# Stage A of six batches on quarters of TensorE

## The chip, the cores and the metric

The kernel runs on one core of one Trainium2 chip. The metric is the device time of one execution in microseconds (us). The kernel before takes 795.54 us, the median of three runs from 795.02 to 796.49 us.

## What is computed

```python
x: (8, 3008, 256)            # batch, sequence, dim
X = np.fft.rfft(x, axis=1)   # along the 3008 rows of each batch
Y = X * (filt_r + 1j * filt_i)
y = np.fft.irfft(Y, n=3008, axis=1)
h = np.maximum(y.reshape(24064, 256) @ w_in, 0.0)   # w_in: 256 x 2048
out = (h * h) @ w_out                               # w_out: 2048 x 256
```

The Fourier transform is done as matmuls. 3008 is 64 times 47, so a batch is first transformed over 47 rows for each of 64 residues n1 ("stage A", into u), then over the 64 residues ("stage B", psB), multiplied by the filter, and brought back in two steps (psP, psY). The two dense layers (psH, then psO) follow.

## The kernel before

Stage A of a batch has a 94-row contraction: the residues n1 are split in two halves h of 32, and a row of the tile x is a pair (n2, h) with n2 below 47. The constant SA holds the cosines and sines of 47 rows twice, each only in the rows of its own h, so half of the 94 x 96 constant is zero. One matmul takes 94 rows, 96 columns and two values of m (512 elements).

```python
for c in range(NC):                       # NC = 24
    for h in range(2):
        SA[:, h, h, 0, c] = np.cos(2 * np.pi * n2 * c / N2)
        SA[:, h, h, 1, c] = np.sin(2 * np.pi * n2 * c / N2)
...
p_x32 = ctx.enter_context(tc.tile_pool(name="p_x32", bufs=2))
p_x16 = ctx.enter_context(tc.tile_pool(name="p_x16", bufs=4))
p_u = ctx.enter_context(tc.tile_pool(name="p_u", bufs=3))
...
def psF(name):
    return pps.tile([128, 512], F32, tag="psF", name=name, bufs=2)
...
def load_x(b, c, pool=None, tag="x32", q=None):
    t = (pool or p_x32).tile([96, 8, D], F32, tag=tag, name=f"x32_{b}_{c}")
    ...                                    # one transfer, two for the last batch
def cast_x(b, c, eng=nc.vector):
    t = p_x16.tile([94, 8, D], F16, tag="x16", name=f"x16_{b}_{c}")
    eng.tensor_copy(out=t, in_=x32s.pop((b, c))[0:94])
    x16s[(b, c)] = t

def write_u(b, c):
    nc.sync.dma_start(
        out=dU[b].rearrange("(m q) d -> q m d", q=96)[:, 8 * c:8 * c + 8, :],
        in_=us.pop((b, c)))

def unit_a(b, a):
    c, i = divmod(a, 4)
    if i == 0:
        us[(b, c)] = p_u.tile([96, 8, D], F16, tag="u", name=f"u_{b}_{c}")
    ps = psF(f"psA_{b}_{a}")
    m = slice(2 * i, 2 * i + 2)
    if b == 1:
        ...                                # batch 1: another layout of x
    else:
        nc.tensor.matmul(ps[0:96, :], sSA, x16s[(b, c)][:, m, :], start=True, stop=True)
    o = us[(b, c)][:, 2 * i:2 * i + 2, :]
    pv = ps[0:96, :].rearrange("p (a d) -> p a d", d=D)
    if a % 2 == 0:
        nc.scalar.copy(out=o, in_=pv)
    else:
        nc.vector.tensor_copy(out=o, in_=pv)
    if i == 3:
        write_u(b, c)
```

u goes out to DRAM (dU) and comes back in another order (ut) for stage B. The main loop has one step for every eighth of a group of 512 tokens. In each step TensorE does the matmuls of the first layer, then what the plan puts in place 0, then the matmuls of the second layer, then place 1:

```python
# fft_plan(b): steps count from the start of the plan of batch b
t0 = 2 if b == 1 else 6
for a in range(12 if b == 1 else 0, 16):
    put(t0 + a // 2, a % 2, unit_a, b, a)          # batches 2 to 7: steps 6 to 13
put(10 if b == 1 else 14, 1, read_u, b)            # dU -> ut
t0 = 14 if b == 1 else 18
for p in range(12):
    r = t0 + (18 if b == 1 else 19) * p // 11
    put(r, 0, unit_b, b, p)                        # stage B from step 18
    ...
for s in range((NG + 1) * SLOTS):
    g, k = divmod(s, SLOTS)
    if g < NG:
        ffn_g1(g, k)          # psH: 4 matmuls of 512 columns; ScalarE: relu into h
    run(work, s, 0)
    if g > 0:
        ffn_g2(g - 1, k)      # psO: 8 matmuls of 256 columns
    run(work, s, 1)
    if g > 0:
        ffn_out(g - 1, k)     # every fourth step: ScalarE copies psO out
    if g < NG:
        ffn_sq(g, k)          # VectorE: h * h
```

Of the kernel before, what the change touches and what calls it, by code (L numbers as in the profile page):

```python
# [9 lines left out]
F16 = mybir.dt.float16  # L10
F32 = mybir.dt.float32
# [7 lines left out]
N1, N2, NC, NM = 64, 47, 24, 32  # L19
# [7 lines left out]
def _build_consts():  # L27
    N = N1 * N2
    n2 = np.arange(N2)
    m = np.arange(NM)  # L30


    SA = np.zeros((N2, 2, 2, 2, NC))
    for c in range(NC):
# [6 lines that stand above are left out]
    S0 = np.zeros((128, 6, 2, 48))  # L41
    for h in range(2):
        q = SA[:, h, h].reshape(N2, 48)
        for t in range(2):
            S0[2 * h + t::4, t, h] = q[:32]
        for c in range(4):
            S0[4 * h + c:120:8, 2 + c, h] = q[32:]


    freq = np.full((NC, 64), -1)  # L50
    for c in range(NC):
        for j in range(32):
            freq[c, j] = 47 * j + c
            if c:
                freq[c, 32 + j] = 47 * j + 47 - c
    freq[0, 32] = N // 2


    SB = np.zeros((NM, 2, 2, NC, 2, 64))

    n1j = 8 * (m % 8) + 2 * (m // 8)
    SP = np.zeros((2, 64, NC, 2, 2, NM))
    for c in range(NC):
        for f in range(64):
            k = freq[c, f]
            if k < 0:
                continue
            sg = 1.0 if (f < 32 or c == 0) else -1.0
            for h in range(2):
                th = 2 * np.pi * ((k * (32 * h + m)) % N) / N  # L70
                SB[:, h, 0, c, 0, f] = np.cos(th)
                SB[:, h, 1, c, 0, f] = -sg * np.sin(th)
                SB[:, h, 0, c, 1, f] = -np.sin(th)
                SB[:, h, 1, c, 1, f] = -sg * np.cos(th)
            if c == 0 and f == 32:
                SB[:, :, 1, c, :, f] = 0.0
            w = (1.0 if k in (0, N // 2) else 2.0) / N
            for i in range(2):
                th = 2 * np.pi * ((k * (n1j + i)) % N) / N
                cs, sn = w * np.cos(th), w * np.sin(th)  # L80
                SP[0, f, c, i, 0] = cs
                SP[0, f, c, i, 1] = sg * sn
                SP[1, f, c, i, 0] = -sn
                SP[1, f, c, i, 1] = sg * cs


    SY = np.zeros((32, 2, 2, N2, 2))
    for c in range(NC):
        th = 2 * np.pi * c * n2 / N2
        for i in range(2):  # L90
            SY[c + c // 12 * 4, i, 0, :, i] = np.cos(th)
            SY[c + c // 12 * 4, i, 1, :, i] = -np.sin(th)


    PF = np.zeros((128, 6, 2, 2, 32))
    for w, (s, q) in enumerate(PQ):
        for j in range(32):
            PF[4 * j + q, w, :, s, j] = 1.0

    f16 = lambda a, p: np.ascontiguousarray(a.reshape(p, -1).astype(np.float16))  # L100
    C0 = np.zeros((128, 1472))
    C0[:, 0:576] = S0.reshape(128, 6, 2, 2, NC).transpose(0, 1, 4, 2, 3).reshape(128, 576)
    C0[:, 576:704] = np.eye(128)
    C0[:, 704:1280] = S0.reshape(128, 576)
    C0[0:94, 1280:1376] = SA.reshape(94, 96)
    C0[:, 1376:1470] = SY.reshape(128, 94)
    return f16(C0, 128), f16(PF, 128), f16(SB, 128), f16(SP, 128)

# [2 lines left out]
def kernel(  # L111
# [9 lines left out]
    nc = tc.nc  # L121
    B, S, D = x.shape
# [17 lines left out]
# [3 lines that stand above are left out]
# [10 lines left out]
    xrows = x.rearrange("b s d -> (b s) d")  # L153
    dU = [dram.tile([NM * 96, D], F16, name=f"dU{b}") for b in range(B)]
    dZ = [dram.tile([NM * 96, D], F16, name=f"dZ{b}") for b in range(B)]

    def psF(name):
        return pps.tile([128, 512], F32, tag="psF", name=name, bufs=2)

    def psO(name):  # L160
        return pps.tile([128, 2, 256], F32, tag="psO", name=name, bufs=2)
# [22 lines left out]
    x32s = {}  # L184

    def load_x(b, c, pool=None, tag="x32", q=None):

        t = (pool or p_x32).tile([96, 8, D], F32, tag=tag, name=f"x32_{b}_{c}")
        q = q or nc.sync
        if b + 1 < B:  # L190
            v = xrows[b * S:b * S + 96 * NM, :].rearrange("(p m) d -> p m d", m=NM)
            q.dma_start(out=t, in_=v[:, 8 * c:8 * c + 8, :])
        else:
            v = xrows[b * S:b * S + S, :].rearrange("(p m) d -> p m d", m=NM)
            q.dma_start(out=t[0:80], in_=v[0:80, 8 * c:8 * c + 8, :])
            q.dma_start(out=t[80:94], in_=v[80:94, 8 * c:8 * c + 8, :])
        x32s[(b, c)] = t


# [1 line left out]
    sC0 = const.tile([128, 1472], F16, name="sC0")  # L201
    nc.scalar.dma_start(out=sC0[:, 0:704], in_=dC0.ap()[:, 0:704])
    s0 = sC0[:, 0:576].rearrange("p (w q) -> p w q", q=96)
    s1 = sC0[:, 704:1280].rearrange("p (w q) -> p w q", q=96)
    sSA = sC0[0:94, 1280:1376]
    sSY = sC0[0:112, 1376:1470]
    ident = sC0[:, 576:704]
    sPF = p_out.tile([128, 6, 128], F16, tag="ost", name="sPF")
# [1 line left out]
    xw32, xw16 = {}, {}  # L210
# [61 lines left out]
    ps = psO("warm").rearrange("p a d -> p (a d)")  # L272
# [61 lines left out]
    x16s, us, uts, prods, zes, zts, yts = {}, {}, {}, {}, {}, {}, {}  # L334

    def cast_x(b, c, eng=nc.vector):
        t = p_x16.tile([94, 8, D], F16, tag="x16", name=f"x16_{b}_{c}")
        eng.tensor_copy(out=t, in_=x32s.pop((b, c))[0:94])  # L338
        x16s[(b, c)] = t

    def write_u(b, c):
        nc.sync.dma_start(
            out=dU[b].rearrange("(m q) d -> q m d", q=96)[:, 8 * c:8 * c + 8, :],
            in_=us.pop((b, c)))

    def unit_a(b, a):

        c, i = divmod(a, 4)
        if i == 0:
            us[(b, c)] = p_u.tile([96, 8, D], F16, tag="u", name=f"u_{b}_{c}")  # L350
        ps = psF(f"psA_{b}_{a}")
        m = slice(2 * i, 2 * i + 2)
        if b == 1:
            nc.tensor.matmul(ps[0:96, :], s1[:, c // 2, :], xw16[(b, 2 * (c % 2))][:, m, :],
                             start=True, stop=False)
            nc.tensor.matmul(ps[0:96, :], s1[0:120, 2 + c, :], xw16[(b, 1)][0:120, m, :],
                             start=False, stop=True)
        else:
            nc.tensor.matmul(ps[0:96, :], sSA, x16s[(b, c)][:, m, :], start=True, stop=True)  # L359
        o = us[(b, c)][:, 2 * i:2 * i + 2, :]  # L360
        pv = ps[0:96, :].rearrange("p (a d) -> p a d", d=D)
        if a % 2 == 0:
# [5 lines that stand above are left out]
# [240 lines left out]
    def fft_plan(b):  # L608

        plan = {}  # L610

        def put(r, place, f, *a):
            plan.setdefault((r, place), []).append((f, a))

        if b == 1:
            for n in range(4, 16):
                put(n if n < 8 else n + 2 if n < 12 else 2 * n - 7, n % 2, unit_y, 0, n)
            for k in range(4):
                put((4, 5, 7, 7)[k], 1, cast_wout, k, nc.vector)
        t0 = 2 if b == 1 else 6  # L620
        for a in range(12 if b == 1 else 0, 16):
            put(t0 + a // 2, a % 2, unit_a, b, a)
        put(10 if b == 1 else 14, 1, read_u, b)
        t0 = 14 if b == 1 else 18
        for p in range(12):
            r = t0 + (18 if b == 1 else 19) * p // 11
            put(r, 0, unit_b, b, p)
            put(r, 0, unit_s, b, p)
            put(r + 2, 1, unit_p, b, p)
        t0 = 35 if b == 1 else 40  # L630
        for c in range(4):
            put(t0, 1, read_z, b, c)
        if b + 1 < B:
            for c in range(2):
                put(t0 - 13, 1, load_x, b + 1, c)
            for c in range(4):
                r = t0 - 8 + 3 * c
                put(r, 1, cast_x, b + 1, c)
                if c < 2:
                    put(r, 1, load_x, b + 1, c + 2)  # L640
        for n in range(16):
            if b == 1:
                put(38 + n // 2 if n > 3 else 39, n % 2, unit_y, b, n)
            else:
                put(44 + n // 2, n % 2, unit_y, b, n)
        return plan
# [16 lines left out]
    for k in range(2):  # L663
        c = slice(12 * k, 12 * k + 12)
# [16 lines left out]
    for k in range(2):  # L681
        sSPx.append(p_u.tile([128, 12, 128], F16, tag="u", name=f"sSPx_{k}"))
        c = slice(12 * k, 12 * k + 12)
# [33 lines left out]
    for c in (0, 2, 1):  # L717
        write_u(1, c)
# [12 lines left out]
    for s in range((NG + 1) * SLOTS):  # L731
        g, k = divmod(s, SLOTS)
# [40 lines left out]
```

## Time and profile before

| what | value |
|---|---|
| time, median of 3 | 795.54 us |
| span of the profiled execution | 795.8 us |
| PE (matmuls) busy | 783.1 us, 98% of the span |
| VectorE (DVE) busy | 552.2 us, 69% |
| ScalarE (ACT) busy | 554.9 us, 70% |
| matmuls of stage A of batches 2 to 7 (psA, line 359) | 96, 382 ns each |
| matmuls of the first layer (psH, line 560) | 1728, 351 ns each |
| matmuls of the second layer (psO, line 577) | 3008, 272 ns each |
| ScalarE's copies of psA to u (line 363) | 50, 572 ns each |
| VectorE's copies of psA to u (line 365) | 50, 687 ns each |
| ScalarE's relu (line 564) | 376, 1025 ns each |

A record of a matmul starts with its reading and has a modelled end, so records of consecutive matmuls overlap: the spacing of their starts, not their length, is what a matmul costs in a full stream. PEld are the loads of the stationary operand. "a <- b" in a row of waits says what the idle engine a waited for.

### The profile page before, as it was taken

How to read it: one execution, taken by the hardware profiler on the slowest of the kernel's cores; microseconds unless marked ns; L12 is line 12 of the kernel's file. 1: busy time of each engine (PE TensorE's matmuls, PEld its weight loads, DVE VectorE, ACT ScalarE, POOL GpSimd, SP SyncE). 2: the span in 40 equal slices, each digit the busy share in tenths (PEclk: the TensorE clock that was granted, in tenths of full speed). 3: DMA queues.
4: the chain of work that ended last, by engine and by line, in shares of the span. 5: the costliest groups of instructions: out<-in, count | busy, mean ns of one | idle time of the engine just before them, and what ended most of it. 6: DMA issues, size and time to landing. Idle time of an engine off the chain costs nothing.

```text
span 795.8 us, 14801 instructions
## 1 busy us (share of the span) xinstructions
PE 783.1 (98%) x6102; PEld 553.7 (70%) x6102; DVE 552.2 (69%) x898; ACT 554.9 (70%) x708; POOL 24.4 (3%) x27
## 2 busy tenths in 40 slices
PE   8989999999999999999999999999999999999998
PEld 5846677667676676867778676776777667776666
DVE  6946995579855897559965699557985589554342
ACT  3856776767777677767777677676776767766664
POOL 3710000000000000000000000000000000000000
PEclk9989999999999999999999999999999999999999
DMA  9994555336724467055471555525563342511111
GB/s 352 361 277 134 130 151 139 92 126 165 202 58 107 158 165 181 30 164 151 124 183 49 171 153 137 129 71 156 156 170 97 87 142 80 123 48 41 40 41 54
DMA packets 88139, 107.32 MB, mean 135 GB/s; under 512 B 6288, under 2 KB 78864, under 8 KB 83856
## 3 DMA queue, kind: packets, MB, share of 16 engines
q1 hardware_dynamic: 87864, 106.19, 46.9%
q8 instruction: 48, 0.79, 0.4%
q10 hardware_dynamic: 144, 0.18, 0.1%
q14 instruction: 19, 0.16, 0.1%
q0 software_dynamic: 64, 0.00, 0.0%
HBM read 58.12 MB, written 48.23 MB: 134 GB/s over the span
## 4 chain that ended last, share of the span: by engine, by line
PE 93%; DMA 3%; ACT 1%; DVE 1%; issue 0%; POOL 0%; SPq 0%; ACTq 0%; DVEq 0%; POOLq 0%
PE psO L577 40%; PE psH L560 39%; PE psA L359 3%; PE psY L530 3%; PE psB L443 2%; PE psP L494 2%; PE warm L274 1%; DMA ut<-dU 1%; DMA xw<-in_x_dram 1%; PE psf L293 1%; DMA dZ<-ze 1%; ACT h L564 1%; PE psf L296 0%; DMA dU<-u 0%; PE psA L380 0%; ACT sF L303 0%
## 5 line engine op out<-in xcount | busy, mean ns | idle before, releaser
L564 ACT ACTIVATE h<-psH 128x1024 f16<-128x1024 f32 x376 | 385.2, 1025 | 189.7 <-PE psH L560 188.2
L577 PE MATMUL psO<-sWout,h 128*128 128x256 f16 x3008 | 388.6, 272 | 0.0
L560 PE MATMUL psH<-yt,sWin 128*128 128x512 f16 (+7 forms) x1728 | 386.9, 351 | 1.7 <-DVE yt L539 0.8
L577 PEld LDWEIGHTS <-h 128*128 128x128 f16 x3008 | 290.6, 98 | 77.3
L568 DVE TENSOR_TENSOR h<-h 128x1024 f16<-128x1024 f16 x376 | 253.7, 685 | 100.8 <-ACT h L564 99.2
L560 PEld LDWEIGHTS <-sWin 128*128 128x128 f16 x1728 | 159.5, 98 | 101.7 <-issue 3.5
L451 DVE TENSOR_TENSOR prod<-psB,sF 128x1024 f16<-128x1024 f32 x84 | 102.4, 1219 | 5.9 <-PE psB L443 5.6
L539 DVE CAST yt<-psY 128x376 f16<-128x376 f32 x62 | 33.9, 549 | 57.4 <-PE psY L530 57.4
L365 DVE CAST u<-psA 96x512 f16<-96x512 f32 x50 | 34.3, 687 | 47.3 <-PE psA L359 45.1
L496 ACT CAST ze<-psP 128x512 f16<-128x512 f32 x84 | 49.2, 586 | 17.8 <-PE psP L494 15.9
L588 ACT COPY ost<-psO 128x512 f32<-128x512 f32 (+1 forms) x96 | 55.7, 580 | 6.7 <-PE psO L577 5.3
L530 PEld LDWEIGHTS <-zt 112*128 112x128 f16 x512 | 34.9, 98 | 12.1 <-issue 2.0
L530 PE MATMUL psY<-sC,zt 112*128 112x94 f16 x512 | 42.3, 205 | 0.6 <-DMA zt<-dZ 0.3
L465 DVE TENSOR_TENSOR yf<-prod,yf 128x512 f16<-128x512 f16 x84 | 35.7, 425 | 2.9
L443 PE MATMUL psB<-ut,sSB 128*128 128x256 f16 x192 | 36.5, 272 | 0.6 <-DMA ut<-dU 0.5
L359 PE MATMUL psA<-x,sC 94*96 94x512 f16 x96 | 36.6, 382 | 0.0
L443 PEld LDWEIGHTS <-sSB 128*128 128x128 f16 x192 | 18.6, 98 | 20.9 <-issue 1.7
L494 PE MATMUL psP<-yf,sSP 128*128 128x256 f16 x168 | 32.1, 273 | 0.2 <-ACT yt L537 0.2
L537 ACT CAST yt<-psY 128x376 f16<-128x376 f32 x66 | 30.7, 468 | 1.1 <-PE psY L530 0.6
L338 DVE CAST x<-x 94x2048 f16<-94x2048 f32 x24 | 29.2, 1216 | 0.0
L363 ACT CAST u<-psA 96x512 f16<-96x512 f32 x50 | 28.6, 572 | 0.0
L458 DVE COPY yf<-prod 64x512 f16<-64x512 f16 x84 | 24.3, 289 | 2.9
(63 smaller groups left out, 255.9 us busy)
## 6 DMA issues: line engine op xcount, KB each, us to landing
x<-in_x_dram SPq DMA_DIRECT2D x20, 768.0 KB
zt<-dZ SPq DMA_DIRECT2D x64, 192.0 KB
dU<-u SPq DMA_DIRECT2D x28, 384.0 KB
dZ<-ze SPq DMA_DIRECT2D x28, 384.0 KB
out_dram<-ost SPq DMA_DIRECT2D x66, 128.0 KB
out_dram<-ost SPq DMA_DIRECT2D x31, 256.0 KB
ut<-dU SPq DMA_DIRECT2D x7, 1024.0 KB
xw<-in_x_dram SPq DMA_DIRECT2D x4, 1024.0 KB
```

The source lines that it names most:

```text
L359: nc.tensor.matmul(ps[0:96, :], sSA, x16s[(b, c)][:, m, :], start=True, stop=True)
L443: nc.tensor.matmul(ps[:, i * D:(i + 1) * D], sSB[:, 2 * p + i, :], uts[b][:, 2 * p + i, :], start=True, stop=True)
L451: nc.vector.tensor_mul(out=prod, in0=ps.rearrange("p (a d) -> p a d", d=D).unsqueeze(1).to_broadcast([128, 2, 2, D]), in1=sF[:, :, 2 * p:2 ...
L465: nc.vector.tensor_add(out=yf, in0=prod[:, 0], in1=yf)
L494: nc.tensor.matmul(ps[:, i * D:(i + 1) * D], sSP[:, 2 * p + i, :], yf[:, i, :], start=True, stop=True)
L496: nc.scalar.copy(out=zes[(b, c)][:, 2 * i6:2 * i6 + 2, :], in_=ps.rearrange("p (a d) -> p a d", d=D))
L530: nc.tensor.matmul(ps[:, 94 * jj:94 * jj + 94], zt[:, 4 * (g % 2) + jj, dt * 128:(dt + 1) * 128], sSY, start=True, stop=True)
L560: nc.tensor.matmul(ps[:, i, o:o + n], sWin[:, dt, jt * 128:(jt + 1) * 128], yts[b][:, dt, r:r + n], start=(dt == 0), stop=(dt == 1))
L564: nc.scalar.activation(out=h2[:, 2 * s:2 * s + 2, :], in_=ps, func=AF.Relu)
L568: nc.vector.tensor_mul(out=v, in0=v, in1=v)
L577: nc.tensor.matmul(pso[g][:, t % 2, :], h2s[g][:, jt, t * 128:(t + 1) * 128], sWout[:, jt, :], start=(jt == 0), stop=(jt == NJT - 1))
L588: nc.scalar.copy(out=ost[:, h0:h0 + step, :], in_=pso[g][:, h0:h0 + step, :])
```

## The change

In batches 2 to 7 the zero half of SA is no longer multiplied. Each half h gets its own 64 rows of the array (rows 0 to 46 and 64 to 110 carry data), and two groups of m go to two halves of the columns (48 of 64 columns carry data). So one pass consists of four matmuls, each on a 64 x 64 quarter of the array, which are meant to run at the same time. A pass computes what two matmuls computed before; there are 8 passes for a batch in place of 16 matmuls. A pass takes both psF buffers, one for each h; ScalarE empties the one, VectorE the other.

For that x is loaded by h: for each of the four chunks two transfers (64 and 48 partitions, 112 in place of 96; the last batch in more pieces), and the cast takes 112 partitions. The tile u has 128 partitions, and write_u makes four transfers of 48 partitions in place of one of 96. In the plan the passes stand in place 0 of steps 6 to 13; place 1 of these steps is empty.

```diff
-    C0[0:94, 1280:1376] = SA.reshape(94, 96)
+    for h in range(2):
+        C0[64 * h:64 * h + N2, 1280:1328] = SA[:, h, h].reshape(N2, 48)
...
-        t = (pool or p_x32).tile([96, 8, D], F32, tag=tag, name=f"x32_{b}_{c}")
+        t = (pool or p_x32).tile([112, 8, D], F32, tag=tag, name=f"x32_{b}_{c}")
...
+        for h in range(2):
+            n = 64 - 16 * h
+            for n0, n1 in ((0, n),) if full else ((0, 32), (32, N2), (N2, n)):
+                a = n0 if full or n0 < N2 else 0
+                q.dma_start(out=t[64 * h + n0:64 * h + n1],
+                            in_=v[h, a:a + n1 - n0, 8 * c:8 * c + 8, :])
...
-    sSA = sC0[0:94, 1280:1376]
+    sSA = sC0[:, 1280:1344]
...
-        t = p_x16.tile([94, 8, D], F16, tag="x16", name=f"x16_{b}_{c}")
-        eng.tensor_copy(out=t, in_=x32s.pop((b, c))[0:94])
+        t = p_x16.tile([112, 8, D], F16, tag="x16", name=f"x16_{b}_{c}")
+        eng.tensor_copy(out=t, in_=x32s.pop((b, c)))
...
+        v = dU[b].rearrange("(m h q) d -> q h m d", h=2, q=48)
+        for k in range(2):
+            for h in range(2):
+                m = 8 * c + 4 * k
+                nc.sync.dma_start(out=v[:, h, m:m + 4, :], in_=u[64 * k:64 * k + 48, h])
+
+    def pass_a(b, a):
+        c, j = divmod(a, 2)
+        if j == 0:
+            us[(b, c)] = p_u.tile([128, 2, 4, D], F16, tag="u", name=f"u_{b}_{c}")
+        ps = [psF(f"psA_{b}_{a}_{h}") for h in range(2)]
+        for k in range(2):
+            for h in range(2):
+                m = 4 * k + 2 * j
+                nc.tensor.matmul(ps[h][64 * k:64 * k + 64, :], sSA[64 * h:64 * h + N2, :],
+                                 x16s[(b, c)][64 * h:64 * h + N2, m:m + 2, :],
+                                 start=True, stop=True)
+        for h, eng in enumerate((nc.scalar.copy, nc.vector.tensor_copy)):
+            eng(out=us[(b, c)][:, h, 2 * j:2 * j + 2, :],
+                in_=ps[h].rearrange("p (a d) -> p a d", d=D))
+        if j == 1:
+            write_u(b, c)
...
-            nc.tensor.matmul(ps[0:96, :], sSA, x16s[(b, c)][:, m, :], start=True, stop=True)
...
-        for a in range(12 if b == 1 else 0, 16):
-            put(t0 + a // 2, a % 2, unit_a, b, a)
+        if b == 1:
+            for a in range(12, 16):
+                put(2 + a // 2, a % 2, unit_a, b, a)
+        else:
+            for a in range(8):
+                put(6 + a, 0, pass_a, b, a)
```

More of the change, by code (lines that the diff above doesn't have):

```diff
@@ L186, in load_x @@
     def load_x(b, c, pool=None, tag="x32", q=None):
-        t = (pool or p_x32).tile([96, 8, D], F32, tag=tag, name=f"x32_{b}_{c}")
+        t = (pool or p_x32).tile([112, 8, D], F32, tag=tag, name=f"x32_{b}_{c}")
         q = q or nc.sync
[L190 to L196, printed above, removed]
+        full = b + 1 < B
+        v = xrows[b * S:b * S + (64 if full else N2) * 64, :].rearrange(
+            "(n h m) d -> h n m d", h=2, m=NM)
+        for h in range(2):
[4 more added lines that the diff above has]
+                            in_=v[h, a:a + n1 - n0, 8 * c:8 * c + 8, :])
         x32s[(b, c)] = t
@@ L336, in cast_x @@
     def cast_x(b, c, eng=nc.vector):
-        t = p_x16.tile([94, 8, D], F16, tag="x16", name=f"x16_{b}_{c}")
-        eng.tensor_copy(out=t, in_=x32s.pop((b, c))[0:94])
+        t = p_x16.tile([112, 8, D], F16, tag="x16", name=f"x16_{b}_{c}")
+        eng.tensor_copy(out=t, in_=x32s.pop((b, c)))
         x16s[(b, c)] = t
     def write_u(b, c):
-        nc.sync.dma_start(
-            out=dU[b].rearrange("(m q) d -> q m d", q=96)[:, 8 * c:8 * c + 8, :],
-            in_=us.pop((b, c)))
+        u = us.pop((b, c))
+        if b == 1:
+            nc.sync.dma_start(
+                out=dU[b].rearrange("(m q) d -> q m d", q=96)[:, 8 * c:8 * c + 8, :], in_=u)
+            return
+        v = dU[b].rearrange("(m h q) d -> q h m d", h=2, q=48)
[19 more added lines that the diff above has]
+            write_u(b, c)
     def unit_a(b, a):
@@ L352, in unit_a @@
         m = slice(2 * i, 2 * i + 2)
[L353 to L359, printed above, removed]
+        nc.tensor.matmul(ps[0:96, :], s1[:, c // 2, :], xw16[(b, 2 * (c % 2))][:, m, :],
+                         start=True, stop=False)
+        nc.tensor.matmul(ps[0:96, :], s1[0:120, 2 + c, :], xw16[(b, 1)][0:120, m, :],
+                         start=False, stop=True)
         o = us[(b, c)][:, 2 * i:2 * i + 2, :]
@@ L619, in fft_plan @@
                 put((4, 5, 7, 7)[k], 1, cast_wout, k, nc.vector)
-        t0 = 2 if b == 1 else 6
-        for a in range(12 if b == 1 else 0, 16):
-            put(t0 + a // 2, a % 2, unit_a, b, a)
+        if b == 1:
+            for a in range(12, 16):
[3 more added lines that the diff above has]
+                put(6 + a, 0, pass_a, b, a)
         put(10 if b == 1 else 14, 1, read_u, b)
```

## The prediction

> **What bounds the kernel now.** I read the busy times first, then the slices of the span, the waits of TensorE, and the chain that ended last around one stage A. The page's first part, and from its second the slices of TensorE and of the clock granted to it:
>
> ```profile
> PE 783.1 (98%) x6102; PEld 553.7 (70%) x6102; DVE 552.2 (69%) x898; ACT 554.9 (70%) x708; POOL 24.4 (3%) x27
> ...
> PE   8989999999999999999999999999999999999998
> ...
> PEclk9989999999999999999999999999999999999999
> ```
>
> TensorE is busy everywhere, at full clock. Its waits are few; after the prologue these two kinds matter, half a microsecond each:
>
> ```profile
> PE psH L560 <- DVE yt L539: 0.8, 2, 0.5
> PE psB L443 <- DMA ut<-dU: 0.5, 1, 0.5
> ```
>
> So a nanosecond of TensorE's stream is a nanosecond of the whole, wherever no new wait appears. The chain of work (start us, us, what) shows a step just after the stage A of batch 2, and steps of the stage A of batch 3:
>
> ```profile
> 159.45 0.87 PE psO L577 x8
> 160.33 0.86 PE psH L560 x4
> 161.19 0.87 PE psO L577 x8
> ...
> 243.77 0.22 PE psA L359
> 243.99 0.88 PE psO L577 x8
> 244.87 0.22 PE psA L359
> 245.08 0.86 PE psH L560 x4
> 245.95 0.22 PE psA L359
> 246.17 0.88 PE psO L577 x8
> ```
>
> Without stage A a step lasts 161.19 - 159.45 = 1.74 us; with it 246.17 - 243.99 = 2.18 us. Two matmuls of psA are the difference, 0.44 us, 0.218 us each. All of stage A that changes is 96 x 0.218 = 20.9 us, or 2.6% of 795.8. This is the sum at stake, and half of it, 10.5 us or 1.3%, is what four quarters running perfectly together could save.
>
> **What the Trainium skill says.** "TensorEngine Tiling (Array Packing)", section Key Properties, says that tiles work independently, but that a change of the tiling mode drains TensorE. Every pass stands alone between psH and psO on the whole array, so there are two changes a pass, 96 in all. The trace before has no pass in tiles, hence no price for this. "TensorE: Matmul & The Clock Gate", section Measured speedup vs the span model, gives 3.07 times for four row tiles and 2.38 for three column tiles, so both kinds of tile do run together, not perfectly. The same page, section The mechanism, says that a weight load overlaps running matmuls only where the row groups differ; in a pass the third load has the row group of the first matmul. No run here shows that yet. The first page, section PSUM Bottleneck, says that tiling does not speed up the emptying of PSUM. The trace agrees that its price goes with elements per partition: 572 ns on ScalarE and 687 on VectorE for 512, and the change leaves 512.
>
> **The change part by part.**
>
> Removed: 96 psA matmuls, -20.9 us.
>
> Added: 48 passes of four matmuls of 512 columns. The streaming of one is 0.216 us (0.86 / 4 of a psH group). Four of them together: with the skill's 3.07, 4 x 0.216 / 3.07 = 0.28 us, an estimate. To that come two changes of mode. A psA record is 382 ns long and its neighbour starts 218 ns later, so 0.16 us of a matmul's record lie beside the next one; a full drain would lay this bare at each change, 0.33 us a pass. I take about 0.06 us at each change, since the wavefront itself should be shorter than the record's tail and part of the reading may be early; this is a choice, not a reading. A pass is then 0.28 + 0.12 = 0.40 us, 48 of them 19.2 us. Sum on TensorE: 19.2 - 20.9 = -1.7 us.
>
> The weight loads rise from 96 to 192, but are within the pass estimate.
>
> Beside TensorE: the copies of psA stay 48 on each engine at 572 and 687 ns, with 128 partitions in place of 96. In a step of stage A ScalarE has 1025 + 572 = 1.60 us, and every fourth step 590 ns more for ost, 1.75 us on the average. A step of 1.74 + 0.40 = 2.14 us holds that, and even 1.97 us, the shortest. A pass needs both psF buffers; the relu starts 0.04 us after the pass's start and takes 1.02, then u 0.57, so ScalarE frees its buffer about 1.6 us after the pass began, before the next pass at 2.1. No new wait. The casts of x take the same elements per partition (1216 ns, 24 times). x grows from 768 to 896 KB a chunk, about 0.4 us of transfer at the 361 GB/s of the page's second slice, well ahead of its use: the plan loads the chunks 26 to 18 steps before stage A and casts them 21 to 12 steps before.
>
> On the path: u. In batch 3 the chain leaves TensorE between stage A and B:
>
> ```profile
> 253.57 0.23 PE psA L359
> ...
> 253.83 0.70 DVE u L365
> ...
> 254.59 3.45 DMA dU<-u
> ...
> 258.44 3.63 DMA ut<-dU
> ...
> 262.11 0.38 PE psB L443 x2
> ```
>
> There is no slack there: stage B's first matmuls wait for ut. After the change the last pass stands where psA stood at 252.48 us. ScalarE's relu and copy of u end 1.53 us later (254.01 in the trace), so the writes start about 0.5 us earlier. But they are four of 96 KB, issued 0.3 us apart on SyncE, so the last is issued 1.0 us after the first. The large one carried data from about 0.85 to 2.9 us after its issue, so four small ones should land 3.4 to 3.9 us after the first. Then 0.4 + 3.63 us as before: ut is there at 252.48 + 1.6 + 3.65 + 4.05 = 261.8 us. TensorE gets to stage B at 252.48 + 0.40 + 5 x 1.74 = 261.6 us. The wait of batch 3 becomes 0.2 us from 0.5, and in the other batches, where now there is hardly any, it could be 0 to 0.4. I add 0.5 us for the six. "DMA: Bandwidth & Descriptors", section Rules for kernel authors, holds that transfers to disjoint halves of the partitions serialize; that speaks for no gain from the split, and no run here shows it.
>
> Sum: -1.7 + 0.5 = -1.2 us, 794.3. Because a perfect overlap is as thinkable as a bad one and the change's own purpose speaks for the first, I say 793.8.
>
> **The rivals.** (1) Changes of mode cost nothing: a pass is 0.23 us, 48 x (0.23 - 0.436) = -9.9 us, 785.6. For it: the trace's weight loads lie wholly beside running matmuls (a psO group of 8 takes 0.87 us with its 8 loads). Against: the skill's drain. (2) Full drains laid bare at both ends: 0.28 + 0.33 = 0.61 us, +8.4 us, 803.9; with one weight load bare after each change (98 ns for a full one, 123 for the psA's) 0.82 us, +18 us, 814. For it: the skill's word, and 0.16 us of tail in the records. (3) The second pair on the other columns waits for the first, because their row groups are the same: 2 x 0.216 in place of 0.28, +0.15 us a pass, +7 us on top of mine, 801. (4) Four small writes take longer than one, and ut comes later by 1 us in each batch: +6 us, 800. For it: there is no slack. Against: the bytes are the same and SyncE's issues are short.
>
> **Range and chances.** The low end is rival 1, the high end rival 2 without bare loads and some of rival 4: 785.5 to 806. A gain over 2% (below 779.6) is more than half of stage A and out of reach of the arithmetic: 0.01. A loss over 2% (above 811.4) needs drains and loads bare in all 96 changes, or two rivals together: 0.05. Within 2%: 0.94.
>
> **What would show it.** In the profile after, the spacing of psO groups in stage A: 2.14 us by my step, 1.97 by rival 1, 2.35 to 2.56 by rival 2. The starts of the four matmuls of a pass: within 0.1 us of one another by mine, in two pairs 0.2 us apart by rival 3. Waits of psB on ut above 1 us in total would be rival 4. A wait of psA on ScalarE or VectorE would prove the buffer step wrong. Steps outside stage A must stay at 1.74 us; if they don't, the whole reckoning is wrong.

## The result

The changed kernel takes 816.16 us (median of 4 runs, 815.16 to 817.08), the kernel before 796.01 us beside it. The ratio is 1.025, with a 95% interval of 1.0225 to 1.0275: slower by more than 2%. The prediction was 793.8 us, 785.5 to 806.0.

The page of the changed kernel, first and second part:

```profile
PE 786.9 (97%) x6198; PEld 545.7 (67%) x6198; DVE 556.5 (68%) x898; ACT 555.2 (68%) x708; POOL 24.2 (3%) x27
...
PE   8989999999999999999999999999959999999998
...
PEclk9999999999999999999999999999988999999999
```

One slice of TensorE has fallen to 5, and the clock dips behind it. The span is 813.5 us, a slice is 20.3 us, so this lies near 600 us. TensorE's waits (engine line waited for: us in total, times, longest us):

```profile
PE psY L558 <- DMA zt<-dZ: 7.6, 6, 5.1
PE psO L605 <- DVE h L596: 5.0, 1, 5.0
PE psB L471 <- DMA ut<-dU: 1.4, 3, 0.7
```

Two single waits of 5 us are new. The wait of psO on VectorE was in nobody's list. And the steps of stage A, at which the change was aimed? The timeline of TensorE (start us, us, what), batch 3:

```profile
248.75 0.38 PE L588 MATMUL psH<-yt,sWin 128*128 128x512 f16 x1
249.06 0.41 PE L368 MATMUL psA<-x,sC 47*64 47x512 f16 x4
249.41 1.05 PE L605 MATMUL psO<-sWout,h 128*128 128x256 f16 x8
...
251.59 1.05 PE L605 MATMUL psO<-sWout,h 128*128 128x256 f16 x8
```

The step lasts 251.59 - 249.41 = 2.18 us, as before. The pass is exactly as dear as the two matmuls that it replaced. The four matmuls, 400 ns each in the records, together span 0.41 us: they start within 0.01 us. But the last psH starts at 248.75 and the pass only at 249.06, 0.31 us later in place of 0.216; and psO starts 0.35 us after the pass, again in place of 0.216.

So stage A brought nothing, and the loss is elsewhere. The first psA of the six batches tells where. Those of batches 6 and 7, in the changed kernel and then in the kernel before (count, least/median/greatest ns, first and last start us):

```profile
L368 PE MATMUL psA<-x,sC x32: 400/400/400, 523.7 to 539.0; 47*64 47x512 f16 x32
L368 PE MATMUL psA<-x,sC x32: 400/400/400, 635.0 to 650.3; 47*64 47x512 f16 x32
...
L359 PE MATMUL psA<-x,sC x16: 381/382/382, 522.8 to 539.2; 94*96 94x512 f16 x16
L359 PE MATMUL psA<-x,sC x16: 381/381/381, 618.3 to 634.6; 94*96 94x512 f16 x16
```

From batch 6 to batch 7 it is 635.0 - 523.7 = 111.3 us, before it was 618.3 - 522.8 = 95.5. That is 15.8 of the 17.7 us by which the spans differ. The chain of work in that stretch leaves TensorE altogether:

```profile
567.79 15.66 DMA x<-in_x_dram
...
587.64 12.07 DMA x<-in_x_dram
...
600.14 8.15 DMA dZ<-ze
...
608.31 3.38 DMA zt<-dZ
...
611.83 0.47 PE psY L558 x4
```

It is the load of x of the last batch, which has shapes of its own: the rows behind n2 = 46 don't exist there, and the change fills partitions 47 to 63 from the batch's first rows, in one transfer of 17 partitions a chunk. VectorE, TensorE and then the DMA, from the timelines and from the busy times by stretch:

```profile
597.44 1.23 DVE L343 CAST x<-x 112x2048 f16<-112x2048 f32 x1 [6.54 <-DMA x<-in_x_dram]
...
606.80 1.23 DVE L343 CAST x<-x 112x2048 f16<-112x2048 f32 x1 [6.33 <-DMA x<-in_x_dram]
```

```profile
599.33 1.21 PE L605 MATMUL psO<-sWout,h 128*128 128x256 f16 x4 [5.01 <-DVE h L596]
600.33 1.91 PE L588 MATMUL psH<-yt,sWin 128*128 128x512 f16 x4
602.04 1.91 PE L605 MATMUL psO<-sWout,h 128*128 128x256 f16 x8
...
611.83 0.47 PE L558 MATMUL psY<-sC,zt 112*128 112x94 f16 x4 [5.08 <-DMA zt<-dZ]
```

```profile
core 0: us, PE busy (x) PEld busy (x) DVE busy (x) ACT busy (x) POOL busy (x), PEclk, DMA share, GB/s
592.00:595.00 3.00, 2.32 (x17) 1.46 (x15) 0.00 (x0) 2.35 (x3) 0.00 (x0) 1.00 0.07 25
601.00:604.00 3.00, 3.00 (x12) 1.66 (x11) 0.00 (x0) 1.02 (x1) 0.00 (x0) 0.50 0.47 152
...
610.00:620.00 10.00, 8.17 (x54) 5.55 (x55) 2.29 (x4) 2.77 (x4) 0.00 (x0) 0.66 0.77 149
```

VectorE stood 6.5 us before a cast, because x was not there; behind the cast in its queue were three squarings of h, and psO needed the first. From 592 to 595 us the transfers moved 25 GB/s at a mean share of 0.07 of 16 engines: one engine, 1/16, at work alone, while VectorE and then TensorE waited for it. The packet records of the stretch say the same: packets of 8 KB one at a time, a new one every 0.31 us. After the 5 us of idling TensorE had half its clock (0.50 from 601 to 604 us): from the four psH at 600.33 to the psO at 602.04 it took 1.71 us in place of 0.86. The same happened again after the wait for zt (mean clock 0.66 from 610 to 620 us). The two waits of 5.0 and 5.1 us leave 5.7 of the 15.8 us for the slow matmuls behind them. That agrees with the clock records: half clock for 6.8 us each time, of which TensorE worked 4.9 and 6.0, so 5.5 us were lost.

The second wait has the same source as far as the trace tells. The last chunk's piece was on its way from 599.4 to about 606 us, again a packet of 8 KB every 0.31 us, and VectorE's next cast waited 6.3 us for it; in the same time the write of dZ, which zt reads, took 8.15 us to land. That this write stood behind the piece is a reading and not a test; the second run below removes both waits together.

"DMA: Bandwidth & Descriptors" of the Trainium skill, section Why a DMA increments its semaphore by 16 and not by 1, states the rule that fits: a transfer is spread over the largest number of engines up to 16 that divides the slowest dimension of both its sides. By that rule 17 partitions give one engine. The trace agrees: a share of 0.07, one packet at a time, and 17 rows of 8 KB, 139 KB, take 5.6 us at 25 GB/s.

### The profile page after: what moved, and what is told of

It is laid out like the page before. It is cut to its first block, busy times and chain, and to the rows that moved or that the text cites. A ratio compares the mean times of both kernels' runs of the same rounds, so it can differ in the third digit from the quotient of the medians.

```text
span 813.5 us, 15179 instructions
## 1 busy us (share of the span) xinstructions
PE 786.9 (97%) x6198; PEld 545.7 (67%) x6198; DVE 556.5 (68%) x898; ACT 555.2 (68%) x708; POOL 24.2 (3%) x27
## 4 chain that ended last, share of the span: by engine, by line
PE 79%; DMA 14%; DVE 3%; ACT 2%; SPq 1%; issue 1%; POOL 0%; ACTq 0%; DVEq 0%; POOLq 0%
PE psO L605 34%; PE psH L588 32%; DMA x<-in_x_dram 4%; DMA dZ<-ze 4%; PE psY L558 3%; DMA zt<-dZ 3%; DMA ut<-dU 2%; PE psB L471 2%; PE psP L522 2%; PE psA L368 2%; PE warm L279 1%; DMA xw<-in_x_dram 1%; DVE h L596 1%; ACT h L592 1%; DMA dU<-u 1%; DVE prod L479 1%
## 5 line engine op out<-in xcount | busy, mean ns | idle before, releaser
L372 DVE CAST u<-psA 128x512 f16<-128x512 f32 x48 | 33.2, 692 | 36.4 <-PE psA L368 36.2
L343 DVE CAST x<-x 112x2048 f16<-112x2048 f32 x24 | 29.3, 1222 | 14.7 <-DMA x<-in_x_dram 14.6
L372 ACT CAST u<-psA 128x512 f16<-128x512 f32 x48 | 27.9, 580 | 0.0
L486 DVE COPY yf<-prod 64x512 f16<-64x512 f16 x84 | 24.3, 290 | 2.9
L487 DVE COPY yf<-prod 64x512 f16<-64x512 f16 x84 | 24.2, 288 | 1.1
```

The costliest lines, as they stand in the source:

```text
L372: eng(out=us[(b, c)][:, h, 2 * j:2 * j + 2, :], in_=ps[h].rearrange("p (a d) -> p a d", d=D))
```

## Experiments

**Theories.** A: the last batch's pieces of 17 partitions cost the time. B: the passes and their changes of mode cost it. C: the number of small transfers does. On the pass itself there are two theories as well: 0.22 us of streaming and 0.22 us for two changes of mode, or four quarters that don't really run together.

**1. The last batch without filler** (e1). The filler, the rows behind n2 = 46, is left out; no matmul reads it. The cast is two of 47 partitions.

```diff
-            for n0, n1 in ((0, n),) if full else ((0, 32), (32, N2), (N2, n)):
+            for n0, n1 in ((0, n),) if full else ((0, 32), (32, N2)):
```

> The changed kernel, but the last batch's x is loaded without the filler rows (pieces of 17 partitions and of 1 partition left out; 4 transfers a chunk in place of 6), and its cast is two of 47 partitions. Theory A, the filler pieces hold up the queue and with it batch 7: the 111 us between the first psA of batch 6 and that of batch 7 fall to about 96, the wait of psO on VectorE (5.0 us) and the long one of psY on zt (5.1 us) go, and the time is 795 to 801 us. Theory B, the passes themselves and their mode changes cost the 20 us: the time stays above 812 us. Theory C, the 15-partition pieces or the number of transfers does it: between, 804 to 812 us.

Measured: 801.21 us, ratio to before 1.0068 (1.0039 to 1.0098). Theory B falls. The two waits of 5 us are gone, and the stretch from batch 6 to batch 7 is 98.7 us; both this and the time lie just above what theory A gave (about 96 us, 795 to 801 us). Two waits of psP on VectorE's yf (1.9 us in total) come with the second cast, which costs VectorE 1.2 us a chunk; the third and fourth run, which have one too, show the same 1.9 us.

**2. The same filler, 17 cut into 1 and 16** (e2). The bytes stay, the transfers become more.

```diff
-            for n0, n1 in ((0, n),) if full else ((0, 32), (32, N2), (N2, n)):
+            for n0, n1 in ((0, n),) if full else ((0, 32), (32, N2), (N2, 48), (48, 64))[:4 - h]:
```

> The changed kernel with the same filler rows in the last batch, but the piece of 17 partitions cut into one of 1 and one of 16 (7 transfers a chunk in place of 6, the same bytes). Theory A1, the piece of 17 is slow because of its odd number of partitions: 795 to 802 us, as without filler. Theory A2, the number of transfers or the bytes of the filler do it: 814 us or more.

Measured: 799.04 us, ratio 1.0036 (1.0025 to 1.0048). One more transfer a chunk, and 17.1 us less than the changed kernel: neither the bytes nor the number of transfers were it, but the 17. The stretch from batch 6 to batch 7 is 620.0 - 524.5 = 95.5 us, exactly as before the change:

```profile
L368 PE MATMUL psA<-x,sC x32: 400/400/400, 524.5 to 539.8; 47*64 47x512 f16 x32
L368 PE MATMUL psA<-x,sC x32: 400/400/400, 620.0 to 635.3; 47*64 47x512 f16 x32
```

This run is the base for what follows. What is left to explain is 0.36%, 2.7 us by the medians. Its waits:

```profile
PE psB L471 <- DMA ut<-dU: 2.5, 3, 1.2
PE psY L558 <- DMA zt<-dZ: 1.8, 4, 0.8
```

**3. The suspect alone in the kernel before** (e3). Four transfers of 17 partitions that nothing needs, and a cast of them.

```diff
             q.dma_start(out=t[80:94], in_=v[80:94, 8 * c:8 * c + 8, :])
+            q.dma_start(out=t[96:113], in_=v[0:17, 8 * c:8 * c + 8, :])
...
+        if b + 1 == B:
+            eng.tensor_copy(out=t[96:113], in_=x32[96:113])
```

> The kernel before with only this added: in the last batch each chunk of x also loads 17 unused partitions of 8 KB, and VectorE casts them too. Theory A: four such pieces alone make it 8 to 18 us slower (804 to 814 us), with VectorE's casts of x waiting on x. Theory C (many small pieces together, or the passes): within 2 us of before.

Measured: 806.66 us, ratio 1.0135 (1.0096 to 1.0173), about 10 us more. psY waits 4.6 us once for zt, TensorE has half its clock behind it (0.50 from 606 to 609 us), and a cast of VectorE waits 2.8 us for x. The stretch from batch 6 to batch 7 is 105.4 us, 9.9 more than in the kernel before. Not all of it is the piece's: 1.9 us are waits for yf, which the added cast makes. And here the piece begins at partition 96, in the changed kernel at 47, so the place where it begins is not what makes it slow. It costs less than in the changed kernel; a likely reason is that here the cast of the real rows doesn't wait for the piece, but no run tests that.

**4. Every pass twice** (e4), on the base of the first run. The second four matmuls write the same values over the first.

```diff
-        for k in range(2):
+        for k in (0, 1, 0, 1):
```

> As the run without filler, but the four matmuls of every pass are done twice in a row (the second time over the first, to the same values), so a pass has eight matmuls and still two changes of mode. If four quarters stream together in 0.22 us and the rest of the 0.43 us of a pass is the two changes, it is 48 x 0.22 = 10 us slower than the run without filler. If the quarters themselves take 0.43 us and changes are free, it is 20 us slower. By my prediction's 0.28 us: 13 us slower.

Measured: 809.91 us, 8.7 us above the run without filler, nearest to the first of the three expectations (10, 13 and 20). TensorE's timeline:

```profile
246.81 0.63 PE L373 MATMUL psA<-x,sC 47*64 47x512 f16 x8
247.37 1.05 PE L610 MATMUL psO<-sWout,h 128*128 128x256 f16 x8
...
249.21 0.63 PE L373 MATMUL psA<-x,sC 47*64 47x512 f16 x8
```

The step is 2.40 us in place of 2.18: four more quarters cost 0.22 us, what one matmul of 512 columns streams. They run together without loss. All the rest of a pass, 0.435 - 0.216 = 0.22 us, is the way in and out. 48 such steps make 10.6 us; the run is 8.7 us slower because TensorE waits less here: psB for ut 0.7 us in place of 1.7, psY for transfers 0.7 in place of 2.1.

**5. Half passes** (e9). Each pass is cut in two halves of two matmuls, one before and one behind psO: the same work with 192 changes of mode in place of 96.

```diff
-                put(6 + a, 0, pass_a, b, a)
+                for k in range(2):
+                    put(6 + a, k, pass_a, b, a, k)
```

> As the run with 16-row filler, but each pass is cut in two half passes of two matmuls (both halves of n1, one group of m), one before and one behind the second layer's matmuls of the step: the same work, 96 half passes and 192 changes of mode. If a half pass streams in 0.22 us like a whole one, with 0.22 us for its two changes, a step of stage A lasts 1.74 + 0.87 = 2.61 us and the run is 48 x 0.435 = 21 us slower than the run with 16-row filler, 818 to 822 us. If a pass's 0.43 us is the work of four quarters and changes are free: 0 to 3 us slower.

Measured: 823.54 us, ratio 1.0344 (1.0318 to 1.037), 24.5 us above the base.

```profile
246.61 0.40 PE L371 MATMUL psA<-x,sC 47*64 47x512 f16 x2
246.94 1.05 PE L610 MATMUL psO<-sWout,h 128*128 128x256 f16 x8
247.92 0.40 PE L371 MATMUL psA<-x,sC 47*64 47x512 f16 x2
248.26 1.04 PE L593 MATMUL psH<-yt,sWin 128*128 128x512 f16 x4
249.23 0.40 PE L371 MATMUL psA<-x,sC 47*64 47x512 f16 x2
```

A step is 249.23 - 246.61 = 2.62 us, as expected: a group of two quarters has the price of one of four. The run is 1.5 us over the range of 818 to 822 us, and lost 3 us more than the 21 of the steps; psB waits 4.2 us for ut here in place of 2.5, the rest of it is not traced.

**6. Two passes at a time** (e6): eight quarters in a row every second step, the second four into a tile of the psH ring, so that a batch has 8 changes of mode in place of 16.

```diff
+        wide = psH(f"psA_{b}_{c}_w")
+        pss = [[psF(f"psA_{b}_{c}_{h}") for h in range(2)], [wide[:, h, :] for h in range(2)]]
+        for j in range(2):
+            ...                        # the four matmuls of pass j into pss[j]
...
-            for a in range(8):
-                put(6 + a, 0, pass_a, b, a)
+            for c in range(4):
+                put(6 + 2 * c, 0, pair_a, b, c)
```

> As the run with 16-row filler, but two passes stand directly behind one another (eight matmuls, the second four into a tile of the psH ring), in steps 6, 8, 10 and 12, so the 48 passes have 48 changes of mode in place of 96. If a pass is 0.22 us of streaming and 0.22 us of two changes, it is 24 x 0.22 = 5.3 us faster than the run with 16-row filler: ratio to the kernel before 0.996 to 0.998, about 793 to 795 us. If the changes are not what costs: no gain, ratio 1.003. Rival: the two pairs of copies of one step hold up the relu, or the psH ring the next step: waits of psH on ScalarE, and no gain.

Measured: 792.97 us, ratio 0.995 (0.9932 to 0.9968). It is faster than both kernels, if only by half a per cent against the kernel before.

```profile
244.44 0.41 PE L367 MATMUL psA<-x,sC 47*64 47x512 f16 x4
244.68 0.39 PE L367 MATMUL psA_w<-x,sC 47*64 47x512 f16 x4
245.00 1.05 PE L604 MATMUL psO<-sWout,h 128*128 128x256 f16 x8
...
248.57 0.41 PE L367 MATMUL psA<-x,sC 47*64 47x512 f16 x4
```

Two steps, one with the pair and one without, last 248.57 - 244.44 = 4.13 us; two steps of 2.18 are 4.36. That is 0.23 us a pair, 24 pairs 5.5 us, and the gain against the base is 6.1. The psH ring and the copies held nothing up: psH waits 0.5 us for ScalarE's h in both. The wait for ut (2.5 us in the base) is no longer among TensorE's waits, which fits the last pair's place, a step earlier; the wait for zt rose from 1.8 to 3.4 us. 5.5 + 2.5 - 1.6 is 6.4 us, against the 6.1 measured.

**7. The same with an earlier read of ut** (e7): `read_u` in step 13 in place of 14.

> As the run with pairs of passes, but the read of ut is placed in step 13 in place of 14. If stage B still waits for ut only because the read stands behind other transfers of SyncE, up to 1 us faster than the pairs; if the four writes of u end the wait, the same within 0.5 us.

Measured: 791.63 us, ratio 0.9944 (0.9924 to 0.9965); against the sixth run the intervals overlap widely. It is the fastest here by its median, but whether the read did it isn't shown: in the sixth run no wait for ut was left that an earlier read could shorten.

**8. and 9. The rest of 0.36%.** The kernel before with u written in four transfers (e8), and the kernel before with x's side alone (e10). Executions of one and the same kernel lie 3 to 5 us apart here, so of effects this small the sign is firmer than the size.

```diff
+        for k in range(2):                              # e8
+            for h in range(2):
+                q, m = slice(48 * h, 48 * h + 48), slice(4 * k, 4 * k + 4)
+                nc.sync.dma_start(out=v[q, 8 * c + 4 * k:8 * c + 4 * k + 4, :], in_=u[q, m, :])
```

> The kernel before with only this changed: in batches 2 to 7 u is written in four transfers of 48 partitions and 4 of m each, as the changed kernel does, in place of one. If the four writes make ut late, psB waits for ut 1.5 to 6 us in total in place of 0.5, and the ratio to before is 1.002 to 1.006. If they don't matter: 0.999 to 1.001.

Measured: 795.16 us, ratio 0.9982 (0.9971 to 0.9993): no loss, rather a small gain. psB does not wait for ut at all: in batches 3 to 5 the last two writes are issued together, and the read follows 2.4 to 2.6 us behind, where it took 3.3 to 3.9 us behind the one write. It is not quite the changed kernel's case: here two of the four can leave before the chunk's last matmuls, there all four need the last pass. So it says that four transfers are not slow in themselves.

```diff
-    C0[0:94, 1280:1376] = SA.reshape(94, 96)            # e10
+    for h in range(2):
+        C0[64 * h:64 * h + N2, 1280:1376] = SA[:, h].reshape(N2, 96)
...                                                      # load_x and cast_x as in e2, sSA on 112 rows
```

> The kernel before with only x's side of the change: x loaded by h on 64 and 48 partitions in two transfers (the last batch cut as in the run with 16-row filler), the cast of 112 partitions, and the same 96 matmuls of 96 columns over 112 rows of which 94 carry weights. The run with 16-row filler is 0.4% slower than before though its passes take as long as the matmuls that they replace; if x's larger and more numerous transfers are the rest, this run is 1.5 to 4 us slower than before (ratio 1.002 to 1.005), with psY waiting 1 to 3 us more for zt. If the rest is on the side of u and the passes: within 1 us of before (0.999 to 1.001).

Measured: 798.44 us, ratio 1.002 (1.0009 to 1.0032), so 0.7 to 2.5 us slower. psY's waits:

```profile
PE psY L534 <- DMA zt<-dZ: 2.1, 4, 1.1
```

Before it was 0.3 us once. x's side makes zt late by about what the base shows (1.8 us); whether by its bytes or by its greater number of transfers isn't separated. The remainder, some 1 us, may be the base's wait for ut of 2.5 us; no run took that away alone. For it the queue of SyncE (start us, us), batch 5, in the base and then in the kernel before:

```profile
445.02 1.78 SPq L356 DMA_DIRECT2D dU<-u  x4
...
450.03 0.81 SPq L462 DMA_DIRECT2D ut<-dU  x2
```

```profile
445.35 0.30 SPq L342 DMA_DIRECT2D dU<-u  x1
...
448.67 0.81 SPq L434 DMA_DIRECT2D ut<-dU  x2
```

From the first write's issue to the read of ut it is 5.0 us in place of 3.3. The four issues alone take 1.8 us. But batch 5 is the worst: in batches 2, 3, 6 and 7 of the base, with the same 1.8 us of issues, it is 3.8 to 4.0 us. So the issues are not all of it, and what makes batches 4 (4.8 us) and 5 late isn't shown.

## Why the prediction was wrong

**The step that failed** is the sentence on x: "x grows from 768 to 896 KB a chunk, about 0.4 us of transfer ..., well ahead of its use". It counted bytes of a full batch and spread them over all engines. The last batch has other pieces; the 17-partition one goes through one engine at 25 GB/s, 5.6 us each, and its cast stands in VectorE's queue before the squarings that TensorE needs. So x was not there ahead of its use: VectorE's cast waited 6.5 us for it, and TensorE twice 5 us. Cutting the 17 into 1 and 16 took 17.1 of the 20.2 us away. The diff showed the piece, `(N2, n)` with N2 = 47 and n = 64; it was not priced, and no rival contained it. The 5% for a slowdown over 2% were given for drains, which did not cause it.

**The pass** was predicted at 0.40 us and measured at 0.435. That these lie close is luck: the sum hid two errors against each other. The quarters were taken at 0.28 us, from a figure for four row tiles; they stream in 0.216 (the run with every pass twice). The two changes of mode were taken at 0.12 us, by choice; they are 0.09 on the way in and 0.13 on the way out, 0.22 together. So the term "-1.7 us" was about 0. The price is neither the whole tail of 0.33 us (rival 2) nor nothing (rival 1). Is it the drain that the Trainium skill states ("TensorEngine Tiling (Array Packing)", Key Properties), or a weight load that lies bare? The loads, before and after (start us, us; in brackets the idle time of weight loading just before):

```profile
244.59 0.12 PEld L359 LDWEIGHTS <-sC 94*96 94x96 f16 x1
244.70 0.38 PE L359 MATMUL psA<-x,sC 94*96 94x512 f16 x1
...
249.06 0.11 PEld L368 LDWEIGHTS <-sC 47*64 47x64 f16 x4 [0.42 <-issue]
```

Before, the load starts 0.11 us ahead of its matmul, beside the psO in front of it. In the pass it starts only with the pass's own first matmul at 249.06, 0.31 us after the last psH: no load runs ahead across the change, and the 0.09 us have gone by before the load begins. That fits a drain on the way in better than a bare load; a run that separates the two is missing. Rival 3 is refuted: the third matmul does not wait for the first, though they share a row group, and the four loads start together. The skill's sentence on row groups and weight loads, cited in the prediction, is not borne out by this pass.

**The wait for ut** was right in kind and too small: +0.5 us for six batches. The changed kernel waits 1.4 us in place of 0.5, which is over the 1 us that the prediction named as the sign of rival 4; the base has 2.5. The read of ut was reckoned to come about 4.05 us after the first write's issue. In the base it came 3.8 to 4.0 us after it in four batches, 4.8 and 5.0 in batches 4 and 5. One term is mis-sized for certain: the last write is issued 1.35 us after the first in place of 1.0. The rest of the delay in the two late batches stays open.

**The range** rested on TensorE's arithmetic and u alone, so its upper end of 806 had no room for a transfer that failed in shape. "Steps outside stage A must stay at 1.74 us" was the right test: batch 6 failed it, and pointed to the cause. The buffer step held: the passes' psA waited for nothing, and the copies took 580 and 692 ns on 128 partitions, hardly more than 572 and 687 on 96.

## What to carry to other kernels

Price a transfer by its number of partitions before its bytes, and look at the last, irregular block first: here one transfer of 17 partitions cost far more than one of 16 and one of 1, and a cast that waits for it blocks whatever stands behind it in its queue. Splitting TensorE into quarters pays by the length of the run in that mode: an entry and an exit together cost as much as one matmul of 512 columns, so four matmuls win nothing over two full ones, and eight win a quarter of a microsecond. When a design has a fixed price for each visit, batch the visits before judging the idea; here, with the 17-partition piece out of the way, the same idea went from +0.4% to -0.5%.

## What the runs showed that was not expected

- The price of entering and leaving the quarters does not depend on what lies between: 0.22 us around two, four or eight quarter matmuls.
- Four 64 x 64 matmuls of 512 columns start within 0.01 us and stream in the time of one; four more behind them add 0.22 us.
- One transfer on 17 partitions ran at 25 GB/s with a DMA share of 0.07, while with the same bytes as 16 + 1 TensorE had neither of the two waits of 5 us.
- Each of the three waits of 4.6 to 5.1 us of TensorE (two in the changed kernel, one in the third run) was followed by half its clock (0.50 from 601 to 604 us in the changed kernel), and what the slow matmuls behind the two waits there lost is about half of the waits themselves.
